# One list schedule for attention and experts, and the carried row added by VectorE

## The chip, the cores and the metric

The kernel runs on one core of one Trainium2 chip. The metric is the device time of one execution in microseconds (us), from a median of several runs. Five engines run side by side, each with a queue of its own that is worked off in order: PE (TensorE, matrix products, with PEld for its weight loads), DVE (VectorE), ACT (ScalarE, functions by tables), POOL (GpSimd) and SP (SyncE, which issues most of the transfers).

## The reference

Inputs are q, k, v, a_re, a_im of shape (4, 8, 768, 48) and the weights of a mixture of 8 experts. First a linear attention with a complex decay per step, head by head:

```python
mag = np.sqrt(a_re * a_re + a_im * a_im)
scale = np.minimum(mag, 0.999) / (mag + 1e-06)
for t in range(S):
    new_re = ar * S_re - ai * S_im
    new_im = ar * S_im + ai * S_re
    S_re, S_im = (new_re + kv, new_im)        # kv = k_t v_t^T
    y[:, :, t] = np.einsum('bhd,bhde->bhe', q[:, :, t], S_re)
```

Its output, seen as x of shape (3072, 384), goes through top-1 experts with a skip test:

```python
do_compute = x @ w_skip > 0
e_idx = np.argmax(xc @ w_gate, axis=1)        # xc = x[do_compute]
h = np.maximum(xc[mask] @ w1[e], 0.0)         # w1[e]: 384 x 1024
y[mask] = gate_w[mask, None] * (h @ w2[e])    # w2[e]: 1024 x 384
out[do_compute] = xc + y
```

## The kernel before

**Attention.** Time is cut into 6 chunks of 128 steps; a unit u is one chunk of one of the 4 batch rows (24 units, u = 4 x chunk + row), always with all 8 heads. The decays become angles and logarithms (`gates`): ScalarE takes Ln and Exp with one table and Arctan and Sin with another, so units are put into batches (`STARTS`) to share table loads. The angle summed up to the end of a chunk is carried: the last row of the reduced angle is moved to partition 0 by a small transfer (L308), GpSimd multiplies it by -2 pi (L312), and GpSimd adds it to the first row of the next chunk's Arctan (L288); then a matrix product with a triangle sums over time. Per unit there follow the products with cos and sin (`w`, L394), transposes (`tp`), copies of them out of PSUM (`wT`, L411; for units 0 to 5 two of four are VectorE's, `SHARE`), scores (`pa`), masked scores (`at`, L441), the state (`st` and `T`, L448 and L461), the output (`py`, `yT`) and its last product (`px`), which puts tokens in rows (`xa`) and gives logits (`lg`).

**Routing.** For each chunk the rank of a token within its expert is found by products with a triangle of ones (`rank`), and the token rows are scattered by an indirect transfer of GpSimd to a table `xs` of 256 rows per expert (`place`, L543). In the last chunk this is done row by row (`route1`), and expert 0 doesn't wait for the table: its tokens are gathered by products with one-hot matrices `ohx`, with the earlier part read back (`early`).

**Order.** `Plan` holds every step of the attention with its engine, its time, its due time, what it needs and which buffers it takes and frees; `Plan.order` is a list scheduler that plays these through and writes one order, and `attention` emits the steps in it, each engine's instruction pinned behind the one before. The experts (`moe`, L859) are written as loops over e, and the framework's own scheduler orders them under a few pins (`issue_after`). Each expert: weights w1 and w2 are loaded (`r`), cast to a high part (`h`, ScalarE, L808) and a low part (`l`, VectorE, L809); tokens `xg` are loaded from `xs` (L826), transposed and split into `xh`, `xl`; 8 x 9 products give `ph` (L889), ReLU splits it into `hh` (ScalarE, L891) and `hl` (VectorE, L892); 2 x 8 x 3 products give `po`; `og` scales and adds (VectorE, L911) and an indirect transfer writes the rows out (L912). A flag (`check`) says whether a fallback is needed.

Of the kernel before, what the change touches and what calls it, by code (L numbers as in the profile page):

```python
# [21 lines left out]
DM = H * D  # L22
# [8 lines left out]
ROOMS = dict(ain=6, tr=5, U=6, cs=2, e=5, qk=4, w0=2, w1=2, wT0=2, wT1=2, vt=3, at=2, st=2, yT=2, row=4, G=1, raw=2,  # L31
             tp=2, pa=2, y=1, g=1, c=2, xa=3)
LEADS = {0: 4.4, 1: 2.53, 2: 4.25, 3: 2.2, 4: 3.8, 5: 3.0, 6: 2.65, 7: 4.06, 8: 4.22}
SHARE = lambda u: ((0, 1), (1, 1)) if u < 6 else ()
# [12 lines left out]
class Plan:  # L47
# [3 lines left out]
    OVER = dict(P=0.0, A=0.085, V=0.085, G=0.0)  # L51
# [4 lines left out]
    def add(self, key, eng, us, at, need=(), take=(), free=()):  # L56
        def put(fn):
            need_ = list(need)
            if (key[0], key[1] - 1) + key[2:] in self.ops and key[0][:2] not in ("rt", "ro"):
                need_.append((None, (key[0], key[1] - 1) + key[2:]))  # L60
            self.ops[key] = (eng, us, at, need_, list(take), fn)
            for x in free:
                self.rel.setdefault(x, []).append(key)
        return put

    def order(self):
        end, free, held, out = {}, dict.fromkeys("PAVGS", 0.0), {"xa": [("xa", "z")]}, []
        pipe, warm = 0.0, [-9.0, 0.0]
        todo = dict(self.ops)

        def ready(eng, need, take):
            t = 0.0
            for x in need:
                x, after = (x[1], False) if x[0] is None else (x, True)
                if x not in end:
                    return None
                f, e, d = end[x]
                t = max(t, d if after and e != eng else f)
            for x in take:
# [7 lines left out]

        while todo:
            can = {}
            for key, (eng, us, at, need, take, fn) in todo.items():  # L90
                r = ready(eng[0], need, take)
                if r is not None:
                    can.setdefault(eng[0], []).append((max(r, free[eng[0]]), at, key))
            assert can, [(k, [y for y in v[3] if y not in end], v[4]) for k, v in todo.items()]
            e, l = min(can.items(), key=lambda x: min(x[1]))
            t0 = min(l)[0] + NEAR
            s, at, key = min((x for x in l if x[0] <= t0), key=lambda x: (x[1], x[0]))
            eng, us, at, need, take, fn = todo.pop(key)
# [16 lines left out]
            out.append((s, key, fn))  # L115
        self.end = end
# [3 lines left out]
class Kern:  # L120
# [108 lines left out]
    def gates(self, u, k, t, end):  # L229
# [18 lines left out]
        @add(("inv", u), "A", 0.54, t, [("ln", u), E], take=[("tr", u)])  # L248
# [4 lines left out]
        @add(("r", u), "V", 0.55, t, [("inv", u)])  # L253
# [3 lines left out]
        @add(("rr", u), "V", 0.63, t, [("r", u)])  # L257
# [4 lines left out]
        @add(("ln1", u), "A", 0.62, t + 0.1, [("rr", u), E])  # L262
# [3 lines left out]
        @add(("sum", u), "V", 0.57, t + 0.1, [("ln1", u)])  # L266
# [4 lines left out]
        @add(("eps", u), "A", 0.62, t + 0.1, [("sum", u), E])  # L271
# [3 lines left out]
        @add(("U", u), "V", 0.55, t + 0.1, [("eps", u)], take=[("U", u)], free=[("ain", u)])  # L275
# [4 lines left out]
        @add(("atan", u), "A", 0.51, t1, [("sum", u), T])  # L280
# [9 lines left out]
        @add(("pt", u), "P", 0.68, t1, [("on" if c else "atan", u)], take=[("c", "pt", u)])  # L290
# [4 lines left out]
        @add(("near", u), "A", 0.485, t1, [("pt", u)])  # L295
# [3 lines left out]
        @add(("y", u), "V", 0.61, t1, [("near", u)], free=[("c", "pt", u)])  # L299
# [4 lines left out]
        if c < NCH - 1:  # L304
# [9 lines left out]
        @add(("abs", u), "V", 0.38, t1, [("y", u)])  # L314
# [3 lines left out]
        @add(("sin", u), "A", 0.52, t1 + 0.1, [("y", u), T], take=[("cs", c)] if b == 0 else [])  # L318
# [5 lines left out]
        @add(("cos", u), "A", 0.61, t1 + 0.1, [("abs", u), ("sin", u), T],  # L324
# [4 lines left out]
        @add(("pl", u), "P", 0.68, t2, [("U", u), ("pt", end - 1)], take=[("c", "pl", u)], free=[("U", u)])  # L329
# [4 lines left out]
        @add(("e0", u), "A", 0.59, t2, [("pl", u), E2], take=[("e", u)])  # L334
# [4 lines left out]
        @add(("e1", u), "A", 0.59, t2, [("e0", u), E2], free=[("c", "pl", u)])  # L339
# [9 lines left out]
    def factors(self, c, t):  # L349
# [3 lines left out]
        @add(("f0", c), "P", 0.25, t, [("dG", c * B + b) for b in range(B)], take=[("g", "f0", c)], free=[("G", c)])  # L353
# [10 lines left out]
        @add(("f2", c), "P", 0.2, t, [("f1", c)], take=[("g", "f2", c)])  # L364
# [8 lines left out]
    def ready(self, u, t):  # L373
# [11 lines left out]
        @add(("qe", u), "V", 0.95, t, [("lq", u), ("e1", u)], free=[("e", u)])  # L385
# [3 lines left out]
        for k in range(2):  # L389
            @add(("w", u, k), "V", 0.95, t, [("qe", u), ("sin", u), ("cos", u)] + ([("w", u, 0)] if k else []),  # L390
# [5 lines left out]
            for hh in range(2):  # L396
                @add(("tp", u, k, hh), "P", 0.45, t, [("w", u, k)], take=[("tp", u, k, hh)], free=[(f"w{k}", u)])
# [8 lines left out]
                @add(("wT", u, k, hh), "V" if onV else "A", 0.68 if onV else 0.587, t, [("tp", u, k, hh)],  # L406
# [10 lines left out]
    def unit(self, u):  # L417
# [12 lines left out]
        for hh in range(2):  # L430
            @add(("pa", u, hh), "P", 0.9, t, [("wT", u, k, hh) for k in range(2)], take=[("pa", u, hh)], free=[("wT1", u)])
# [5 lines left out]
            @add(("at", u, hh), "V", 0.68, t, [("pa", u, hh)], take=[("at", u)], free=[("pa", u, hh)])  # L437
# [6 lines left out]
        if c > 0:  # L444
            @add(("Sb", u), "V", 0.55, t, [("T", u - B), ("f3", c - 1)], take=[("st", u)])
# [4 lines left out]
        if not late:  # L450
            @add(("ps", u), "P", 1.39, t, [("w", u, 1), ("lv", u)], take=[("g", "ps", u)], free=[("w1", u), ("vt", u)])
# [13 lines left out]
        for hh in range(2):  # L465
            @add(("py", u, hh), "P", 1.09 if c else 0.55, t,
# [14 lines left out]
        @add(("yT", u), "A", 0.585, t, [("py", u, 0), ("py", u, 1)], take=[("yT", u)], free=[("y", u)])  # L481
# [6 lines left out]
        @add(("px", u), "P", 0.74, t, [("yT", u), ("wg", 0)], take=[bank], free=[("yT", u)])  # L488
        def _():
            xs = [H // 2, 2 * D + E + 1]  # L490
            px = X["px", u] = self.bank(f"px_{nm}", xs) if late else self.ps_g.tile([128] + xs, F32, name=f"px_{nm}", tag="g")
            for hp in range(H // 2):
                pe = PE.matmul(px[:, hp], X["yT", u][:, hp], self.wg[:, hp], start=True, stop=True)
            self.px_ins = pe.ins
# [13 lines left out]
        @add(("xa", u), "A", 0.485, t, [("px", u), ("lg", u)], free=[bank])  # L508
# [3 lines left out]
        if late or b == B - 1:  # L512
            @add(("ox", u), "S1", 1.0 if late else 4.0, t + 0.3, [("xa", u)], free=[("xa", c)])
# [11 lines left out]
    def chain(self, name, at, steps, *need):  # L525

        last = list(need)
        for i, (eng, us, fn, *more) in enumerate(steps):
            self.plan.add((name, i), eng, us, at, last + list(more))(fn)
            if eng != "A":  # L530
# [83 lines left out]
    def route1(self, c, b, at):  # L614
# [14 lines left out]
        def rank():  # L629
            R["pr"] = self.ps_g.tile([128, E], F32, name=f"pr_{c}_{b}", tag="g")  # L630
            PE.matmul(R["pr"], self.tri, R["oh"], start=True, stop=False)
            self.pr_ins[b] = PE.matmul(R["pr"], self.ones, self.ohs, start=False, stop=True).ins
# [23 lines left out]
        if b == 0:  # L656
            self.plan.add(("early", 0), "S1", 2.0, at, [(f"rt{c - 1}", 19 + B)], take=[("xa", "early")])(self.early)
# [465 lines left out]
```

## Time and profile before

| | us |
|---|---|
| runs: median of 3 | 438.28 (437.83 to 438.39) |
| profiled execution | 437.74, its span 435.5 |
| PE busy, PEld busy | 384.3, 346.2 |
| DVE busy | 325.4 |
| ACT busy | 282.7 |
| POOL busy | 120.6 |

The attention takes the first 280 us and the experts the rest. Busy time of PE is modelled at its ends and matmuls overlap, so a busy PE is not a PE at its peak; that of DVE and ACT is one instruction after the other. "granted clock" (PEclk) is the share of TensorE's full 2.4 GHz that it was given: 1.00 or 0.50 (1.2 GHz), and a mean between them over a stretch with both.

### The profile page before, as it was taken

What the parts mean: (1) busy time and instruction counts of PE and PEld (TensorE: products, weight loads), DVE (VectorE), ACT (ScalarE), POOL (GpSimd) and SP (SyncE); (2) the same over time, 40 slices, a digit from 0 to 9 for tenths busy, and PEclk for the clock granted to TensorE, in tenths of its full rate; (3) what the DMA queues carried; (4) which work ended last, traced back from release to release, by engine and by line L of the source; (5) the groups of instructions that cost most, each with busy time, mean ns of one, the idle gap of its engine ahead of it and who ended that gap; (6) DMA issues with size and microseconds to landing.
All of it is one profiled execution on the core that took longest, in us unless ns stands there. A gap on an engine that the chain in (4) does not pass through costs nothing. (4 is left out here: it accounts for less than half of the span.)

```text
span 435.5 us, 8846 instructions
## 1 busy us (share of the span) xinstructions
PE 384.3 (88%) x3236; PEld 346.2 (79%) x3236; DVE 325.4 (75%) x714; ACT 282.7 (65%) x540; POOL 120.6 (28%) x134
## 2 busy tenths in 40 slices
PE   0557989799999898898999989897899999999993
PEld 0246779588889687687789888896899999999993
DVE  4479999996989989898889866569555857668321
ACT  5798977779799899889876552267345645655120
POOL 7024324403452531572350041201210202012011
PEclk9976999999999999999999999999699999999998
DMA  9999768576749925531485522497746667465000
GB/s 159 186 149 171 130 115 217 206 171 141 143 129 169 145 46 141 90 79 32 129 219 132 175 74 83 129 327 243 244 130 223 195 202 276 149 241 177 2 25 32
DMA packets 148049, 65.55 MB, mean 151 GB/s; under 512 B 129323, under 2 KB 143407, under 8 KB 148000
## 3 DMA queue, kind: packets, MB, share of 16 engines
q1 hardware_dynamic: 145440, 60.29, 57.9%
q0 software_dynamic: 2560, 4.63, 3.0%
q8 instruction: 28, 0.46, 0.5%
q14 instruction: 21, 0.17, 0.1%
HBM read 52.33 MB, written 15.77 MB: 156 GB/s over the span
## 5 line engine op out<-in xcount | busy, mean ns | idle before, releaser
L809 DVE TENSOR_TENSOR l<-r,h 128x768 fp32r<-128x768 f32 (+1 forms) x56 | 58.1, 1068 | 10.0 <-ACT h L808 9.8
L808 ACT CAST h<-r 128x768 fp32r<-128x768 f32 (+1 forms) x56 | 49.9, 925 | 19.0 <-DMA r<-in_moe_w_dram 8.3
L402 PE MATMUL tp<-ident,w 128*96 128x128 f32 x384 | 54.8, 283 | 7.8 <-ACT wT L411 4.9
L889 PE MATMUL ph<-xh,h 128*128 128x256 f32 x192 | 54.2, 288 | 3.5 <-DVE hl L892 3.2
L891 ACT ACTIVATE hh<-ph 128x256 fp32r<-128x256 f32 x64 | 23.4, 380 | 51.8 <-PE ph L889 51.8
L402 PEld LDWEIGHTS tp<-ident,w 128*96 128x96 f32 x384 | 42.9, 131 | 16.1 <-ACT wT L411 6.2
L889 PE MATMUL ph<-xh,l 128*128 128x256 f32 x192 | 54.0, 286 | 0.0
L435 PE MATMUL pa<-wT,wT 96*128 96x128 f32 x384 | 51.4, 280 | 1.8 <-ACT wT L411 1.8
L889 PE MATMUL ph<-xl,h 128*128 128x256 f32 x192 | 52.0, 286 | 0.0
L288 POOL TENSOR_TENSOR tr<-tr,row 1x384 f32<-1x384 f32 x20 | 30.7, 1554 | 73.7 <-ACT tr L222 68.0
L435 PEld LDWEIGHTS pa<-wT,wT 96*128 96x128 f32 x384 | 47.4, 194 | 4.2 <-ACT wT L411 2.2
L411 ACT COPY wT<-tp 96x512 f32<-96x512 f32 x84 | 46.0, 581 | 6.2 <-PE tp L402 6.1
L394 DVE TENSOR_TENSOR w<-qk,cs 128x768 f32<-128x768 f32 x48 | 47.5, 1004 | 0.4 <-PE tp L402 0.2
L892 DVE SCALAR_TENSOR_TENSOR hl<-ph,hh 128x256 fp32r<-128x256 f32 x64 | 25.7, 418 | 29.1 <-ACT hh L891 29.0
L543 POOL DMA_INDIRECT xs<-xa,sl x24 | 29.5, 1229 | 63.4 <-ACT yT L484 38.0
L912 POOL DMA_INDIRECT out_dram<-og,idx x16 | 20.0, 1249 | 91.5 <-DVE og L911 75.3
L906 PE MATMUL po<-h,hh 128*128 128x384 f32 x128 | 43.4, 340 | 0.0
L907 PE MATMUL po<-l,hh 128*128 128x384 f32 x128 | 42.8, 336 | 0.0
L312 POOL TENSOR_SCALAR row<-row 1x384 f32<-1x384 f32 x20 | 28.7, 1434 | 44.2 <-DMA row<-tr 43.4
L908 PE MATMUL po<-h,hl 128*128 128x384 f32 x128 | 40.4, 337 | 0.0
L889 PEld LDWEIGHTS ph<-xh,h 128*128 128x128 f32 x192 | 37.0, 193 | 3.8 <-DVE hl L892 3.4
L476 PE MATMUL py<-at,vt 128*64 128x128 f32 x384 | 37.5, 281 | 2.1 <-ACT tr L222 1.1
(160 smaller groups left out, 853.8 us busy)
## 6 DMA issues: line engine op xcount, KB each, us to landing
r<-in_moe_w_dram SPq DMA_DIRECT2D x24, 512.0 KB
r<-in_moe_w_dram SPq DMA_DIRECT2D x32, 384.0 KB
ain<-in_a_re_dram SPq DMA_DIRECT2D x24, 192.0 KB
ain<-in_a_im_dram SPq DMA_DIRECT2D x24, 192.0 KB
qk<-in_q_dram SPq DMA_DIRECT2D x24, 192.0 KB
qk<-in_k_dram SPq DMA_DIRECT2D x24, 192.0 KB
vt<-in_v_dram SPq DMA_DIRECT2D x24, 192.0 KB
out_dram<-xa SPq DMA_DIRECT2D x5, 768.0 KB
```

Of the source, the lines that this page charges most:

```text
L288: nc.gpsimd.tensor_tensor(first, first, X["row", u - B], ALU.add)
L394: V.tensor_tensor(n, X["qk", u][:, k].unsqueeze(2).to_broadcast([128, H, 2, D]), X["cs", c][:, b], ALU.mult)
L402: nc.tensor.transpose(tp[:, h], n[:, hh * 4 + h].rearrange("p k d -> p (k d)"), self.ident)
L411: (V.tensor_copy if onV else A.copy)(X["wT", u, k][:, hh * 4:hh * 4 + 4], X["tp", u, k, hh])
L435: PE.matmul(pa[:, h % 4], X["wT", u, 1][:, h], X["wT", u, 0][:, h], start=True, stop=True)
L476: PE.matmul(py[j * 64:j * 64 + 64, hp], vt[:, 2 * hp + j], at[:, 2 * hp + j], start=True, stop=(c == 0))
L808: P.append((load, lambda ks=ks, r=r, hi=hi: nc.scalar.copy(hi[:, ks], r[0]), lambda ks=ks, r=r, hi=hi, lo=lo: nc.vector.tensor_tensor(lo[: ...
L809: lambda ks=ks, r=r, hi=hi, lo=lo: nc.vector.tensor_tensor(lo[:, ks], r[0], hi[:, ks], ALU.subtract)))
L889: pe = PE.matmul(ph, w[:, k, js], x[:, k], start=(n == 0), stop=(n == len(terms) - 1))
L906: PE.matmul(po, hh[:, j, sl], w2h[:, j], start=(j == 0), stop=False)
L907: PE.matmul(po, hh[:, j, sl], w2l[:, j], start=False, stop=False)
L908: pe = PE.matmul(po, hl[:, j, sl], w2h[:, j], start=False, stop=(j == NF - 1))
```

## The change

The experts' steps become operations of the same `Plan`: weights, gathers, products, splits, outputs and scatters, the flag's chain and the remainder of the last chunk's routing, each with a time, a due time, its needs and its buffers. `emit` writes the order in two passes, since the experts' pools open when the attention's close, and pins each engine's instruction behind the one before over both. Expert 1's raw weights now use the two buffers of expert 0 and come before the attention's end; from expert 2 on there are four. GpSimd's two operations on the carried row become one of VectorE. The table of numbers is new: 7 batches, other leads, no shared copies (`SHARE` is empty), measured times for many steps; transfers count about half the time.

```diff
-STARTS = [0, 3, 7, 10, 11, 13, 17, 20]
-AHEAD, TRIG, READY, PULL = 3.0, 1.08, 1.49, 2.06
+STARTS = [0, 3, 7, 11, 15, 18, 21]
+AHEAD, TRIG, READY, PULL = 3.0, 0.63, 1.05, 3.44
+WAFTER, WGAP, CHECK = 0.75, 0.21, 2
-SHARE = lambda u: ((0, 1), (1, 1)) if u < 6 else ()
+SHARE = lambda u: ((0, 1), (1, 1)) if u < 0 else ()
...
-            @add(("on", u), "G", 1.4, t1, [("atan", u), ("row", u - B)], free=[("row", u - B)])
+            @add(("on", u), "V", 0.554, t1, [("atan", u), ("mv", u - B)], free=[("row", u - B)])
             def _():
                 first = X["tr", u][0:1, 0]
-                nc.gpsimd.tensor_tensor(first, first, X["row", u - B], ALU.add)
+                V.scalar_tensor_tensor(first, X["row", u - B], -2 * math.pi, first, ALU.mult, ALU.add)
...
-            @add(("row", u), "G", 1.35, t1, [("mv", u)])
-            def _():
-                nc.gpsimd.tensor_scalar(X["row", u], X["row", u], -2 * math.pi, None, ALU.mult)
...
+    def weights(self, e, t, gap, need=(), begin=None):
+        raw_ = "raw" if e < 2 else "raw2"
+        for i in range(KD + NF // 2):
+            old = [] if e < 2 else [("ph", e - 2, NF - 1)] if i < KD else [("po", e - 2, 1, NF - 1)]
+            @add(("wd", e, i), "S1", 1.5 if i < KD else 1.15, t + gap * i, ..., take=[(raw_, e, i)])
+            @add(("wh", e, i), "A", 1.05 if i < KD else 0.835, t + gap * (i + 0.4), [("wd", e, i)] + old)
+            @add(("wl", e, i), "V", 1.22 if i < KD else 0.957, t + gap * (i + 0.4), [("wh", e, i)], free=[(raw_, e, i)])
+
+    def experts(self):
+        T0, TE = n + 1.0, 1.8
+        self.weights(1, n - 1.5, 0.15, [("w", u, 1)])
...
+            te = T0 + TE * e
+            @add(("xg", e), "S1", 1.1, te - 0.9, [("px", u)] + [(f"re{b}", 8) for b in range(B)], take=[("xg", e)])
+                @add(("hl", e, j), "V", 0.418, te + j * 0.11, [("hh", e, j)], free=[("mph", e, j)])
+            if e + 2 < E:
+                self.weights(e + 2, te + WAFTER, WGAP)
+        self.check(T0 + TE * CHECK)
```

What the order is now, at three places. The first is GpSimd and VectorE where the carried row is added for units 11 and following (`tr` is a unit's angles, `row` the carried row, `xs` the scatter of tokens, `T` the state, `qk` a unit's q and k). Before, on POOL:

```order
L288 TENSOR_TENSOR tr_10_995<-tr_10_995,row_6_500 1x384
L543 DMA xs_113<-xa_0_584,sl_0_983 2048x386
L312 TENSOR_SCALAR row_10_1160<-row_10_1160 1x384
L543 DMA xs_113<-xa_0_584,sl_0_983 2048x386
L288 TENSOR_TENSOR tr_11_1198<-tr_11_1198,row_7_904 1x384
L288 TENSOR_TENSOR tr_12_1204<-tr_12_1204,row_8_953 1x384
```

Now, on DVE:

```order
L308 SCALAR_TENSOR_TENSOR tr_11_1113<-row_7_1002,tr_11_1113 1x384
L308 SCALAR_TENSOR_TENSOR tr_12_1193<-row_8_1026,tr_12_1193 1x384
L308 SCALAR_TENSOR_TENSOR tr_13_1237<-row_9_1032,tr_13_1237 1x384
L308 SCALAR_TENSOR_TENSOR tr_14_1287<-row_10_1036,tr_14_1287 1x384
L477 TENSOR_TENSOR T_2_0_1448<-st0_153,ps_2_0_1418 96x384
L322 SCALAR_TENSOR_TENSOR tr_11_1113<-tr_11_1113,col_74,pt_11_1440 128x384
L332 TENSOR_SCALAR tr_11_1113<-tr_11_1113 128x384
L322 SCALAR_TENSOR_TENSOR tr_12_1193<-tr_12_1193,col_74,pt_12_1445 128x384
```

The addition of the row left POOL, whose only work in the body is now the scatters, and four of them stand in a row on DVE ahead of the state sum and the reduced angles (L322) of the same batch.

The second is VectorE at the start of expert 0 (names end in the expert, then j or the part: `l3_1` is the low part of w1 of expert 1, `l8_1` of w2; `xl_0` the tokens' low part; `ok`, `fl` the flag). Before:

```order
L856 TENSOR_TENSOR xl_0_3519<-pt_0_1_3521,xh_0_3518 128x3x128
L809 TENSOR_TENSOR l3_1_3479<-r3_1_0_3482,h3_1_3478 128x1024
L892 SCALAR_TENSOR_TENSOR hl_0_3557<-ph_0_0_3558,hh_0_3556 128x256
L892 SCALAR_TENSOR_TENSOR hl_0_3557<-ph_0_1_3570,hh_0_3556 128x256
L892 SCALAR_TENSOR_TENSOR hl_0_3557<-ph_0_2_3582,hh_0_3556 128x256
L809 TENSOR_TENSOR l3_1_3479<-r3_1_1_3486,h3_1_3478 128x1024
L809 TENSOR_TENSOR l3_1_3479<-r3_1_2_3490,h3_1_3478 128x1024
L892 SCALAR_TENSOR_TENSOR hl_0_3557<-ph_0_3_3594,hh_0_3556 128x256
L809 TENSOR_TENSOR l8_1_3481<-r8_1_0_3494,h8_1_3480 128x768
```

Now:

```order
L815 TENSOR_TENSOR l8_1_3499<-r8_1_3_3476,h8_1_3498 128x768
L688 TENSOR_SCALAR m_5_3_3379<-m_5_3_3379 128x1
L689 RECIPROCAL xa_5_3117<-m_5_3_3379 128x1
L691 SCALAR_TENSOR_TENSOR todo_109<-m_5_3_3379 128x1
L387 COPY Fall_106<-pf_5_3423 96x32
L943 MEMSET ok_3516 128x384
L872 TENSOR_TENSOR xl_0_3513<-pt_0_0_3465,xh_0_3512 128x3x128
L872 TENSOR_TENSOR xl_0_3513<-pt_0_1_3469,xh_0_3512 128x3x128
L956 TENSOR_SCALAR ok_3516<-Fall_106 96x192
L957 TENSOR_SCALAR ok_3516<-Fall_106 96x192
L815 TENSOR_TENSOR l8_1_3499<-r8_1_4_3501,h8_1_3498 128x768
L958 TENSOR_REDUCE fl_3518<-ok_3516 128x1
```

After these come one more split of w2 and then hl_0 for j = 0. The three splits of expert 1's w1 and the first of its w2 moved ahead of expert 0's tokens, and the flag moved from expert 1 to expert 0.

The third is SP's queue there (`r` are raw weights, `xg` tokens from the table). Before, expert 2's tokens stood behind all its weights:

```order
L806 DMA r3_2_0_3732<-in_moe_w1_dram 128x1024
L806 DMA r3_2_1_3736<-in_moe_w1_dram 128x1024
L806 DMA r3_2_2_3740<-in_moe_w1_dram 128x1024
L806 DMA r8_2_0_3744<-in_moe_w2_dram 128x2x384
L806 DMA r8_2_2_3748<-in_moe_w2_dram 128x2x384
L806 DMA r8_2_4_3752<-in_moe_w2_dram 128x2x384
L806 DMA r8_2_6_3756<-in_moe_w2_dram 128x2x384
L826 DMA xg_2_3875<-xs_113 128x2x386
```

Now, from expert 1's second load of w2 on:

```order
L803 DMA r8_1_4_3501<-in_moe_w2_dram 128x2x384
L803 DMA r8_1_5_3510<-in_moe_w2_dram 128x2x384
L850 DMA xg_0_3537<-xs_113 128x2x386
L803 DMA r8_1_6_3550<-in_moe_w2_dram 128x2x384
L803 DMA r3_2_0_3556<-in_moe_w1_dram 128x1024
L850 DMA xg_1_3568<-xs_113 128x2x386
```

Expert 1's tokens now stand behind the first of expert 2's weights, and expert 2's (not shown) behind all of expert 2's and two of expert 3's.

## Rows read from the trace of the kernel before

**Rows 1.** Stages: length, busy us of PE, PEld, DVE, ACT, POOL; PEclk, DMA share, GB/s.

```profile
24.00:60.00 36.00, 28.24 (x188) 22.65 (x189) 34.29 (x60) 32.20 (x64) 15.31 (x11) 0.81 0.83 143
60.00:240.00 180.00, 169.48 (x1642) 144.89 (x1640) 162.22 (x356) 148.75 (x290) 66.29 (x50) 1.00 0.61 136
301.00:315.00 14.00, 9.55 (x58) 9.16 (x57) 9.80 (x22) 5.73 (x12) 4.23 (x3) 0.76 0.79 256
315.00:428.00 113.00, 113.00 (x800) 112.44 (x799) 66.28 (x108) 50.98 (x94) 15.90 (x18) 1.00 0.48 157
```

**Rows 2.** Groups by line, 24 to 262 us: busy us, mean ns | idle before.

```profile
L394 DVE TENSOR_TENSOR w<-qk,cs 128x768 f32<-128x768 f32 x48 | 47.5, 1004 | 0.4 <-PE tp L402 0.2
L411 ACT COPY wT<-tp 96x512 f32<-96x512 f32 x84 | 46.0, 581 | 6.2 <-PE tp L402 6.1
L288 POOL TENSOR_TENSOR tr<-tr,row 1x384 f32<-1x384 f32 x20 | 30.7, 1554 | 73.7 <-ACT tr L222 68.0 <-DVE wT L411 5.7
L741 ACT ACT_TABLE_LOAD x14 | 18.0, 1283 | 0.2
L448 DVE TENSOR_TENSOR st<-T,Fall 96x384 f32<-96x384 f32 x20 | 14.0, 702 | 2.8 <-PE py L479 2.7
L278 DVE SCALAR_TENSOR_TENSOR U<-ain 128x384 f32<-128x384 f32 x21 | 11.3, 548 | 0.0
L411 DVE COPY wT<-tp 96x512 f32<-96x512 f32 x12 | 8.1, 679 | 0.4 <-PE tp L402 0.4
```

**Rows 3.** Timeline around 143 us: start, us, instruction, count.

```profile
142.76 5.85 POOL L288 TENSOR_TENSOR tr<-tr,row 1x384 f32<-1x384 f32 x4 [9.17 <-ACT tr L222]
143.51 2.98 DVE L394 TENSOR_TENSOR w<-qk,cs 128x768 f32<-128x768 f32 x2
146.41 1.35 DVE L448 TENSOR_TENSOR st<-T,Fall 96x384 f32<-96x384 f32 x1
```

**Rows 4.** Timeline at 96 us, DVE.

```profile
96.40 0.95 DVE L394 TENSOR_TENSOR w<-qk,cs 128x768 f32<-128x768 f32 x1
97.27 0.55 DVE L448 TENSOR_TENSOR st<-T,Fall 96x384 f32<-96x384 f32 x1
```

**Rows 5.** Timeline, the end of the attention and the first product of expert 0.

```profile
267.25 0.69 DVE L441 TENSOR_TENSOR at<-pa,mask 128x512 f32<-128x512 f32 x1 [0.72 <-PE pa L435]
...
280.67 0.39 PE L889 MATMUL ph<-xh,h 128*128 128x256 f32 x1 [0.29 <-ACT xh L855]
```

**Rows 6.** Groups by line, 281 to 429 us.

```profile
L889 PE MATMUL ph<-xh,h 128*128 128x256 f32 x192 | 54.2, 288 | 3.5 <-DVE hl L892 3.2 <-ACT xh L855 0.3
L809 DVE TENSOR_TENSOR l<-r,h 128x768 fp32r<-128x768 f32 (+1 forms) x49 | 50.6, 1068 | 8.6 <-ACT h L808 8.4
```

**Rows 7.** Timeline, expert 2's tokens: issue, and the transposes that wait for them.

```profile
302.86 0.37 SPq L826 DMA_DIRECT2D xg<-xs  x1
...
307.54 1.52 PE L842 MATMUL pt<-ident,xg 128*128 128x128 f32 x6 [1.21 <-DMA xg<-xs]
```

**Rows 8.** Busy time by stage, 308 to 312 us.

```profile
308.00:312.00 4.00, 4.00 (x20) 4.00 (x20) 1.88 (x6) 1.35 (x3) 0.00 (x0) 0.50 0.98 380
```

**Rows 9.** Timeline, output steps of experts 4 and 5, two products 1.06 us apart, last product.

```profile
332.40 0.28 PE L889 MATMUL ph<-xh,h 128*128 128x256 f32 x1
333.46 0.28 PE L889 MATMUL ph<-xh,h 128*128 128x256 f32 x1
378.47 0.62 DVE L911 SCALAR_TENSOR_TENSOR og<-po,xg 128x384 f32<-128x384 f32 x1 [1.09 <-PE po L908]
396.01 1.14 DVE L911 SCALAR_TENSOR_TENSOR og<-po,xg 128x384 f32<-128x384 f32 x2 [1.09 <-PE po L908]
428.09 0.34 PE L908 MATMUL po<-h,hl 128*128 128x384 f32 x1
```

**Rows 10.** Timeline, one load of 384 KB: issue, and the cast that waits for it.

```profile
238.31 0.37 SPq L806 DMA_DIRECT2D r<-in_moe_w_dram  x1
...
240.45 0.83 ACT L808 CAST h<-r 128x768 fp32r<-128x768 f32 x1 [1.29 <-DMA r<-in_moe_w_dram]
```

More of the change, by code (lines that the diff above doesn't have):

```diff
@@ L68, in order, with start @@
         pipe, warm = 0.0, [-9.0, 0.0]
-        todo = dict(self.ops)
-        def ready(eng, need, take):
+        left, users, base, todo = {}, {}, {}, set()
+        for key, (eng, us, at, need, take, fn) in self.ops.items():
+            names = {x[1] if x[0] is None else x for x in need}
+            left[key] = len(names)
+            for x in names:
+                users.setdefault(x, []).append(key)
+        def start(key):
+            eng, us, at, need, take, fn = self.ops[key]
             t = 0.0
@@ L74, in ready @@
                 x, after = (x[1], False) if x[0] is None else (x, True)
-                if x not in end:
-                    return None
                 f, e, d = end[x]
-                t = max(t, d if after and e != eng else f)
-            for x in take:
+                t = max(t, d if after and e != eng[0] else f)
+            base[key] = t
+            todo.add(key)
+        def ready(key):
+            t = base[key]
+            for x in self.ops[key][4]:
                 had = held.get(x[0], [])
@@ L115, in order @@
             out.append((s, key, fn))
+            for x in users.get(key, ()):
+                left[x] -= 1
+                if not left[x]:
+                    start(x)
+        assert len(out) == len(self.ops), sorted((k for k in self.ops if k not in end), key=str)[:9]
         self.end = end
@@ L430, in unit @@
         for hh in range(2):
-            @add(("pa", u, hh), "P", 0.9, t, [("wT", u, k, hh) for k in range(2)], take=[("pa", u, hh)], free=[("wT1", u)])
+            @add(("pa", u, hh), "P", 0.91, t, [("wT", u, k, hh) for k in range(2)], take=[("pa", u, hh)], free=[("wT1", u)])
             def _(hh=hh):
@@ L703, in attention, with emit @@
             self.late(0)
-            self.x, self.pr_ins, self.W, self.rests = {}, {}, {}, []
+            self.x = {}
             self.pieces()
-            seen = nc.cur_bb.bb.instructions
-            prev = {}
-            order = self.plan.order()
-            for i, (s, key, fn) in enumerate(order):
-                self.at(24.0 * i / len(order))
-                n0 = len(seen)
-                with ExitStack() as st:
-                    for x in prev.values():
-                        st.enter_context(tc.issue_after(x))
-                    fn()
-                for x in seen[n0:]:
-                    prev[x.engine] = x
-            n = B * NCH
-            self.at(n + 0.5)
-            for r in self.rests:
-                for _ in r:
-                    pass
-            self.at(n + 1)
+            self.order = self.plan.order()
+            self.done, self.prev = {}, {}
+            self.emit(lambda key: key not in self.second)
+    def emit(self, which):
+        seen = self.nc.cur_bb.bb.instructions
+        first, prev = {e: list(v) for e, v in self.done.items()}, {}
+        for i, (s, key, fn) in enumerate(self.order):
+            if not which(key):
+                continue
+            self.at(48.0 * i / len(self.order))
+            n0 = len(seen)
+            with ExitStack() as st:
+                for e in set(first) | set(prev):
+                    before = [x for k, x in first.get(e, ()) if k < i][-1:] + [prev[e] for _ in range(e in prev)]
+                    for x in before:
+                        st.enter_context(self.tc.issue_after(x))
+                fn()
+            for x in seen[n0:]:
+                prev[x.engine] = x
+                self.done.setdefault(x.engine, []).append((i, x))
     def phase_of(self, c):
@@ new lines, in _ @@
+                    for i, (w, x, k) in enumerate(terms):
+                        PE.matmul(ph, w[:, k, ks(j)], x[:, k], start=(i == 0), stop=(i == len(terms) - 1))
+                @add(("hh", e, j), "A", 0.381, te + j * 0.11, [("ph", e, j)], take=[("hh", e)])
+                def _(e=e, j=j):
+                    if ("hh", e) not in X:
+                        X["hh", e], X["hl", e] = [self.hp.tile([128, NF, CAP], F32R, name=f"{a}_{e}", tag=a) for a in ("hh", "hl")]
+                    A.activation(X["hh", e][:, j], X["ph", e, j], AF.Relu)
```

412 lines of the change are left out of this document (196 added, 216 removed).

## The prediction

> **What bounds the kernel now.** I read the busy times by stage first [rows 1]. From 24 to 240 us, the body of the attention, VectorE is busy 34.29 of 36 us and then 162.22 of 180 us (95% and 90%). ScalarE has 32.20 and 148.75 (89% and 83%). TensorE shows 169.48 of 180, but its ends are modelled and its instructions overlap; its weight loads have 144.89 (80%). So I take VectorE as the engine that paces the attention. From 315 us on TensorE is busy all of 113 us: the experts run at its rate, and VectorE (66.28) has room. Between the two stands 301 to 315 us with TensorE busy 9.55 of 14 us at a granted clock of 0.76: that is a hole.
>
> By the Trainium skill, "Perfetto Trace Analysis", section "Identifying the Most-Contended Engine", TensorE's headroom is judged by its weight loads and not by its matmul row, and the busiest engine is the one to relieve. The trace agrees on the first part as far as 80% against 90% can show it; on the second the rule speaks against this change, which puts an operation on that busiest engine.
>
> Second, the groups of the attention by line, with whom each waits for [rows 2], then single instructions in time [rows 3 to 5]. For the hole: what the experts' first products wait for [rows 6, 7], the clock there [rows 8], and the steady period of one expert [rows 9].
>
> **The change, part by part. First the carried row.** GpSimd's two operations for each of 20 units go (L288 alone 30.7 us, mean 1554 ns), and VectorE gets one scalar-times-tensor-plus-tensor of 384 elements for each. Its nearest row is L278, the same form at 128 partitions: 548 ns [rows 2]. That is 20 x 0.548 = +11.0 us on VectorE. Only one partition works, so it could cost less; the bounds are 0.15 us (about what VectorE's smallest operations take, an estimate) and 0.61, so +3 to +12. I take the row of the same length.
>
> Gone too is what GpSimd's operations did to VectorE. A chain of four L288 lasts from 142.76 for 5.85 us; under it two products w took 2.98 us together and the state product st 1.35 [rows 3]. Without GpSimd beside them they take 0.95 and 0.55 [rows 4]. Over the attention the means are 1004 and 702 ns [rows 2]: 48 x 0.054 + 20 x 0.152 = 2.6 + 3.0 = 5.6 us that VectorE loses now. I count all of it as won, -5.6; the bounds are 0 (if the scatters that stay on GpSimd do the same) and -7.
>
> The Trainium skill, "SBUF — State Buffer", section "Who interferes with whom", says why: a VectorE instruction with two SBUF inputs and a GpSimd instruction that reads SBUF take the same port, and the second to issue waits for the whole of the first. The trace agrees: w and st have two SBUF inputs, and 2.98 us for two w of 0.95 holds such a wait.
>
> **Copies.** The 12 transposed copies that VectorE took (L411, 679 ns) go to ScalarE: -8.1 us on VectorE, +12 x 0.581 = +7.0 on ScalarE. Seven batches in place of eight save two table loads, 2 x 1.283 = -2.6 [rows 2]. ScalarE is +4.4 on 180.95 of 216 us; it stays under VectorE, whose work hides it. If that cover is gone the 4.4 us count.
>
> VectorE's sum: +11.0 - 5.6 - 8.1 = **-2.7 us**, taken one to one, since the engine is busy nine tenths (bounds -12 to +4).
>
> **The other order.** Units, loads and batches stand elsewhere on every queue. What this gains or loses the trace of before can't price exactly. A bound: if 60 to 240 us were as full as 24 to 60, VectorE's 17.8 us of idle time would shrink to 9: -9. On the other side the new VectorE operation waits for ScalarE's Arctan, a wait that GpSimd bore 68.0 us of [rows 2]. In the order four of them stand in a row; everything behind them on VectorE (the state sum, the angles, the next masked products) waits too. I take 0 and keep both ends.
>
> **The end of the attention.** From the end of the last masked product (267.25 + 0.69) to the first product of expert 0 (280.67) are 12.7 us [rows 5]. In it TensorE's order was: last px, gathers of rows 0 and 1, ranks of row 2, gather 2, early gather, ranks of row 3, gather 3. Now the ranks of row 2 and gather 0 stand ahead of the last px, and the ranks of row 3 ahead of two gathers, so their wait is filled with gathers. Laid end to end with the durations that the same steps have in this trace (estimates: py 1.9, ranks 0.3, five gathers of about 1.4, px 0.9, copy 0.8, small gaps) I get about 11.3: **-1.4 us** (bounds -3 to +1: two weight splits of 1.2 us now stand in the same stretch of VectorE, ahead of row 3's logits).
>
> **The experts.** From 280.67 [rows 5] to the last product's end at 428.43 are 147.8 us; the steady period is 396.01 - 378.47 = 17.54, eight of them 140.3 [rows 9]. So 7.4 us are lost, all before 315: TensorE stood 3.2 us for VectorE's hl [rows 6], 1.21 for the load of expert 2's tokens, issued at 302.86 [rows 7], and the rest, 3.0, is the half clock after these stalls (0.50 from 308 to 312 [rows 8]). The cause is VectorE's queue: expert 1's splits, which could only start once the attention's buffers were gone, stood between expert 0's activations, and expert 2's and the flag's reductions ahead of expert 1's. In the new order four of expert 1's seven splits stand before expert 0's first xl. What is left: two splits (1.07 us each [rows 6]) and three flag operations ahead of the first hl, which then ends some 4 us after the first product, where the fourth product wants it after 3 x 1.06 = 3.2 (the distance of two hidden columns' first products, 332.40 to 333.46 [rows 9]). I put 0.8 us for that, 0.6 for six later experts at 0.1 (two splits after the output stand ahead of each first hl), and 1.0 for loads that arrive late: expert 1 has two raw buffers, a load of 384 KB took from 238.31 to 240.45, 2.1 us, and a load of tokens 4.7 us, from 302.86 to 307.54 [rows 7, 10]. Together 2.4 in place of 7.4: **-5.0 us** (bounds 0 to -7).
>
> **Sum.** -2.7 - 1.4 - 5.0 = -9.1. The profiled execution took 437.74 us (435.5 of span and 2.2 around it); so 428.6. The median of the runs is 0.5 above it: about **429.1 us**.
>
> **The rivals.** A is the forecast, 424.5 to 433.5.
> B: TensorE paces the attention after all, and VectorE's relief is worth nothing. For it: 169.48 of 180 us busy [rows 1]. Against: VectorE's own stretches without a gap. 437.7 - 6.4 + 0.5 = 431.8.
> C: the order packs VectorE better, up to the -9 above: 420. For it: 24 to 60 us is that full already. Against: that stretch has no routing and no late chunk.
> D: the loads undo the experts' gain. Splits of expert 1 stand ahead of the first hl on VectorE and their casts ahead of it on ScalarE; with two buffers each load starts only when an earlier split is done. At 4.7 us instead of 2.1 for each of two loads the first hl is some 4 to 5 us later, the clock falls again: the gain shrinks to about 0, so 434.
> E, the other side: VectorE waits for Arctan. Six batches carry a row. If VectorE comes to its block when the table load begins, it stands for 1.283 us and the Arctans (an estimate of 0.5 each), some 3 us for four: 6 x 3 = 18, less the 9.1: 447. It decides from 9.1 / 6 = 1.5 us per block on. For it: the 68 us of [rows 2], and the block of four in the order. Against: GpSimd waited because it had nothing else, and ScalarE has the table load well ahead of the block.
>
> **How the numbers follow.** A 0.45, B 0.14, C 0.18, D 0.11, E 0.12. Faster or slower counts beyond 0.2%, 0.9 us, about what runs of this kernel (437.83 to 438.39) can tell. A, B, C are faster, D mostly; 0.83. The near ends of D and E give 0.05 for the same; 0.12 slower. The range, 418 to 438, leaves out the far part of E and of C, and takes in the bounds of VectorE's sum.
>
> **What would show it.** Right: w near 0.95 and st near 0.55 us all through; the new operation near 0.55 and with little wait in front; from first product to last 142 to 143 us, no stretch at half clock after 285 us. Wrong: a wait of VectorE on Arctan over 1.5 us per batch (E); gaps of TensorE ahead of hl or of expert 1's or 2's transposes (D); VectorE less busy than 85% from 60 to 240 with the time unchanged (B). I would be most wrong if the new order left some engine standing at a place that this trace does not have.

## The result and the profile after

The changed kernel takes 425.54 us (median of 4 runs, 425.20 to 426.13) against 438.05 us (435.37 to 438.39): a ratio of 0.973, 95% interval 0.969 to 0.977. The forecast was 429.1 us. The profiled execution took 426.13 us, of which 424.4 are span, so 11.1 us of span went.

First the stages, as in [rows 1]: stretch, length, busy us (instructions) of PE, PEld, DVE, ACT and POOL, granted clock, DMA share, GB/s. The last row is the body of the attention, from 24 us to the end of the last masked product.

```profile
24.00:60.00 36.00, 34.25 (x221) 27.21 (x222) 30.41 (x58) 33.40 (x67) 0.00 (x0) 0.81 0.89 149
60.00:240.00 180.00, 176.00 (x1721) 150.48 (x1720) 162.59 (x384) 151.85 (x303) 22.42 (x20) 1.00 0.62 135
301.00:315.00 14.00, 14.00 (x96) 13.74 (x97) 10.41 (x16) 7.71 (x13) 2.13 (x3) 1.00 0.51 159
24.00:259.68 235.68, 227.56 (x2118) 193.33 (x2120) 210.85 (x505) 196.01 (x388) 28.88 (x27) 0.97 0.67 145
```

The hole at 301 us is gone (14.00 of 14 us, clock 1.00). Before, the body lasted to 267.94 us [rows 5]; the same stretch there, 24.00 to 267.94:

```profile
24.00:267.94 243.94, 224.25 (x2121) 192.10 (x2123) 215.37 (x472) 193.81 (x378) 86.92 (x66) 0.97 0.62 135
```

So the body is 8.3 us shorter: VectorE has 4.5 us less of work (215.4 to 210.9), and its time without work fell by 3.7, from 28.6 to 24.8. The groups behind the 4.5, from 24 to 258 us, which answer to [rows 2]:

```profile
L410 DVE TENSOR_TENSOR w<-qk,cs 128x768 f32<-128x768 f32 x48 | 45.3, 951 | 0.2
L464 DVE TENSOR_TENSOR st<-T,Fall 96x384 f32<-96x384 f32 x20 | 10.9, 548 | 0.5 <-PE py L495 0.5
L308 DVE SCALAR_TENSOR_TENSOR tr<-row,tr 1x384 f32<-1x384 f32 x20 | 10.0, 540 | 0.7 <-ACT tr L242 0.7
L427 ACT COPY wT<-tp 96x512 f32<-96x512 f32 x96 | 52.1, 580 | 2.8 <-PE tp L418 2.6
L332 DVE TENSOR_SCALAR tr<-tr 128x384 int32<-128x384 int32 x21 | 7.6, 361 | 2.0
```

The last of these in the kernel before, from 24 to 262 us:

```profile
L316 DVE TENSOR_SCALAR tr<-tr 128x384 int32<-128x384 int32 x21 | 8.5, 405 | 2.2
```

w fell from 1004 to 951 ns and st from 702 to 548, the values that they have without GpSimd beside them [rows 4]. The new operation takes 540 ns and waited 0.7 us in all 20 places together. VectorE's copies are gone. The step that drops the sign of the reduced angle (L332, before L316) went from 405 to 361 ns. Together these are 10.0 - 8.1 - 2.2 - 3.1 - 0.9 = -4.3 us of the 4.5.

Then the way from the last masked products to expert 0, and to the end:

```profile
258.40 1.28 DVE L457 TENSOR_TENSOR at<-pa,mask 128x512 f32<-128x512 f32 x2
...
270.86 0.39 PE L886 MATMUL ph<-xh,h 128*128 128x256 f32 x1 [0.29 <-ACT xh L868]
...
416.65 0.34 PE L909 MATMUL po<-h,hl 128*128 128x384 f32 x1
```

The end of the attention takes 270.86 - 259.68 = 11.2 us in place of 12.7. The experts take 416.99 - 270.86 = 146.1 in place of 147.8: 1.6 us, where the forecast had 5.0. What TensorE waits for there, from 268 us on, and single waits and transposes of it in time:

```profile
L886 PE MATMUL ph<-xh,h 128*128 128x256 f32 x192 | 54.6, 288 | 1.1 <-DVE hl L896 0.8 <-ACT xh L868 0.3
L862 PE MATMUL pt<-ident,xg 128*128 128x128 f32 x42 | 5.9, 276 | 1.7 <-DMA xg<-xs 1.7
```

```profile
275.69 0.39 PE L886 MATMUL ph<-xh,h 128*128 128x256 f32 x1 [0.78 <-DVE hl L896]
282.44 0.74 PE L862 MATMUL pt<-ident,xg 128*128 128x128 f32 x5 [0.56 <-DMA xg<-xs]
294.30 0.42 SPq L850 DMA_DIRECT2D xg<-xs  x1
301.00 0.85 PE L862 MATMUL pt<-ident,xg 128*128 128x128 f32 x6 [0.55 <-DMA xg<-xs]
330.57 0.28 PE L886 MATMUL ph<-xh,l 128*128 128x256 f32 x1
330.79 0.39 PE L886 MATMUL ph<-xh,h 128*128 128x256 f32 x1
331.01 0.28 PE L886 MATMUL ph<-xl,h 128*128 128x256 f32 x1
355.32 0.85 PE L862 MATMUL pt<-ident,xg 128*128 128x128 f32 x6 [0.36 <-DMA xg<-xs]
373.54 0.85 PE L862 MATMUL pt<-ident,xg 128*128 128x128 f32 x6 [0.20 <-DMA xg<-xs]
```

Three things are to be seen. Each expert takes longer than the steady period of before, 17.54 us [rows 9]: from transposes to transposes 373.54 - 355.32 = 18.2 us, and 17.9 to 18.6 over the others. Expert 2's tokens, issued at 294.30, could be transposed only at 301.00, 6.7 us later. And the rows at 330 us show a loss that stands under no wait: products ph follow each other every 0.12 us, but two here after 0.22.

### The profile page after: what moved, and what is told of

It reads as the page before. It is cut to its first block, busy times and chain, and to the rows that moved or that the text cites. A ratio compares the mean times of both kernels' runs of the same rounds, so it can differ in the third digit from the quotient of the medians.

```text
span 424.4 us, 8790 instructions
## 1 busy us (share of the span) xinstructions
PE 388.5 (92%) x3236; PEld 346.3 (82%) x3236; DVE 319.3 (75%) x722; ACT 283.9 (67%) x550; POOL 56.6 (13%) x94
## 5 line engine op out<-in xcount | busy, mean ns | idle before, releaser
L810 ACT CAST h<-r 128x768 fp32r<-128x768 f32 (+1 forms) x56 | 50.8, 926 | 38.5 <-issue 19.8
L558 POOL DMA_INDIRECT xs<-xa,sl x24 | 28.9, 1206 | 231.3 <-ACT tr L242 85.0
L427 ACT COPY wT<-tp 96x512 f32<-96x512 f32 x96 | 52.1, 580 | 2.8 <-PE tp L418 2.6
L451 PE MATMUL pa<-wT,wT 96*128 96x128 f32 x384 | 52.4, 284 | 0.1
L892 ACT ACTIVATE hh<-ph 128x256 fp32r<-128x256 f32 x64 | 24.3, 383 | 40.1 <-PE ph L886 40.1
L410 DVE TENSOR_TENSOR w<-qk,cs 128x768 f32<-128x768 f32 x48 | 45.3, 951 | 0.2
L909 PE MATMUL po<-h,hl 128*128 128x384 f32 x128 | 43.0, 336 | 0.0
L457 DVE TENSOR_TENSOR at<-pa,mask 128x512 f32<-128x512 f32 x48 | 32.6, 684 | 7.8 <-PE pa L451 7.7
L886 PEld LDWEIGHTS ph<-xh,l 128*128 128x128 f32 x192 | 36.6, 191 | 0.0
L313 PE MATMUL pt<-tr,turns 128*128 128x384 f32 x48 | 22.1, 563 | 15.3 <-ACT tr L242 14.9
```

The costliest lines, as they stand in the source:

```text
L410: V.tensor_tensor(n, X["qk", u][:, k].unsqueeze(2).to_broadcast([128, H, 2, D]), X["cs", c][:, b], ALU.mult)
L427: (V.tensor_copy if onV else A.copy)(X["wT", u, k][:, hh * 4:hh * 4 + 4], X["tp", u, k, hh])
L451: PE.matmul(pa[:, h % 4], X["wT", u, 1][:, h], X["wT", u, 0][:, h], start=True, stop=True)
L457: V.tensor_tensor(X["at", u][:, hh * 4:hh * 4 + 4], X["pa", u, hh], self.mask.rearrange("p (o t) -> p o t", o=1).to_broadcast([128, 4, C]) ...
L810: nc.scalar.copy(X["W", e, n][0][:, ks], X["raw", e, i])
L886: PE.matmul(ph, w[:, k, ks(j)], x[:, k], start=(i == 0), stop=(i == len(terms) - 1))
```

## The experiments

The runs were timed in three groups, each beside the kernel before, whose medians there were 437.62, 438.06 and 438.16 us. Differences marked with a sign are against the changed kernel's 425.54, which was timed beside a 438.05 of the kernel before and not again in these groups: half a microsecond of such a difference can be that of the groups. Stages are those of one profiled execution, which can lie up to 3 us from the median of its run.

**The carried row back on GpSimd, order kept.** `V.scalar_tensor_tensor(first, ...)` becomes `nc.gpsimd.tensor_tensor(...)`, the multiplication stands behind the small transfer; every other instruction is in its place.

```diff
-V.scalar_tensor_tensor(first, X["row", u - B], -2 * math.pi, first, ALU.mult, ALU.add)
+nc.gpsimd.tensor_tensor(first, first, X["row", u - B], ALU.add)
```

> The changed kernel with the carried row back on GpSimd (its two operations), every other instruction in the same place on its engine. Theory 1 (VectorE's busy time paces the attention, and GpSimd's operations cost it nearly what the new operation costs): VectorE loses 20 x 0.54 = 10.8 us and gets back about 7.7 of waits on w and st, so 3 us less of work: 422 to 425. Theory 2 (what the change won is the latency: GpSimd's 1.55 us per row, four in a chain, holds up TensorE's prefix sums and with them each batch): 6 batches of some 1 to 1.5 us, 431 to 435.

Measured: 432.49 us (431.55 to 432.79), +7.0. The body, in the columns of the stages:

```profile
24.00:265.07 241.07, 228.27 (x2118) 193.96 (x2120) 210.55 (x485) 196.76 (x389) 79.98 (x68) 0.96 0.65 142
```

One group of VectorE in it, first with the row on GpSimd, then in the changed kernel:

```profile
L592 DVE TENSOR_TENSOR cand<-lg,mx 128x32 f32<-128x32 f32 x5 | 1.8, 354 | 0.2
```

```profile
L592 DVE TENSOR_TENSOR cand<-lg,mx 128x32 f32<-128x32 f32 x5 | 1.0, 192 | 0.2
```

And the waits along the chain behind the row, from 26 us to the end of the body (us in total, times, longest): the weight load of the prefix sum for the added row, ScalarE's rounding for the sum, VectorE's reduced angle for the rounding. Again with the row on GpSimd and then in the changed kernel:

```profile
PEld pt L313 <- POOL tr L308: 4.2, 5, 1.4
ACT tr L317 <- PE pt L313: 5.0, 10, 1.1
DVE tr L322 <- ACT tr L317: 6.0, 6, 2.4
```

```profile
PEld pt L313 <- DVE tr L308: 1.4, 5, 0.6
ACT tr L317 <- PE pt L313: 1.9, 7, 0.5
DVE tr L322 <- ACT tr L317: 1.9, 3, 0.9
```

VectorE's work is the same, 210.6 against 210.9: the 20 operations that it lost are made up by others that take longer beside GpSimd, small ones too (cand, 354 ns against 192; L332, 440 against 361). The loss is idle time, 30.5 against 24.8, and 4.1 of the 5.7 us are VectorE's wait for the rounding (L322 behind L317), which TensorE's prefix sum and GpSimd's addition precede. Theory 2 holds.

**The copies back on VectorE, order kept.**

```diff
-(V.tensor_copy if onV else A.copy)(X["wT", u, k][...], ...)
+(V.tensor_copy if u < 6 and hh else A.copy)(X["wT", u, k][...], ...)
```

> The changed kernel with 12 of the 24 transposed copies of units 0 to 5 back on VectorE, every instruction in the place that it has on ScalarE in the order. Theory 1 (VectorE paces, as the prediction put it): 12 x 0.68 = 8.1 us more on VectorE, nine tenths of it in the end: 432 to 434. Theory 2 (ScalarE and TensorE are as near to the bound there, so that VectorE's time counts by half or less): 426 to 429.

Measured: 432.36 us (431.40 to 434.01), +6.8; the body is 243.9 us with 217.6 of VectorE's work (+6.7). Theory 1 holds here.

**The old batches and leads.**

```diff
-STARTS = [0, 3, 7, 11, 15, 18, 21]
+STARTS = [0, 3, 7, 10, 11, 13, 17, 20]
```

(with AHEAD to PULL and LEADS of before)

> The changed kernel with the old batches (8) and the old leads, all else as changed (durations, carried row on VectorE, no shared copies, experts in the plan). Theory 1 (the 3.9 us of VectorE's idle time that went, and which the prediction had put at 0, came from the table): two table loads more on ScalarE and those 3.9 us: 429 to 434. Theory 2 (they came from the row and the copies, whatever the table): 425 to 427.

Measured: 431.65 us (430.84 to 432.42), +6.1, in the range of theory 1. But the reason is not the one expected: the body has 215.7 us of VectorE's work (+4.9) and 26.6 of other time. Some 3.7 us of the work are three more splits of weights, which in this order fall ahead of the end of the last masked product, and the experts are 1.0 us shorter (145.1). So of the new table's 6.1 us only 1.8 show as VectorE's idle time; more lies in what the order puts ahead of the attention's end.

**Four accumulators for ph.**

```diff
-mph=3, mpo=3
+mph=4, mpo=2
```

> The changed kernel with four accumulators for ph and two for po in place of three and three. Theory 1 (the experts' steady period is 17.95 in place of 17.54 because VectorE's splits stand ahead of the first hl, and TensorE then waits for an accumulator): the 0.78 us wait in expert 0 and some 0.2 to 0.35 us in each of six experts go, 422.5 to 424. Theory 2 (the longer period has another cause, the late loads of tokens alone, or the wait only moves to po): 425 to 426.

Measured: 426.04 us (423.23 to 427.36), no change that can be told. The waits of TensorE from 270 us on:

```profile
L886 PE MATMUL ph<-xh,h 128*128 128x256 f32 x192 | 53.8, 284 | 0.3 <-ACT xh L868 0.3
L862 PE MATMUL pt<-ident,xg 128*128 128x128 f32 x42 | 5.9, 277 | 3.8 <-DMA xg<-xs 3.7
```

The wait for hl is gone, as theory 1 said, and of the 16 products that followed after about 0.22 us 3 are left; but the wait for tokens grew from 1.7 to 3.7 us. The experts take 146.2 us, as in the changed kernel (146.1). The time was taken by the next one in line, as theory 2 had it.

**Three token buffers**, and then **both**.

```diff
-xg = X["xg", e] = self.xp.tile([128, 2, XW], F32, name=f"xg_{e}", tag="xg")
+xg = X["xg", e] = self.xp.tile([128, 2, XW], F32, name=f"xg_{e}", tag="xg", bufs=3)
-@add(("xg", e), "S1", 1.1, te - 0.9, ...)
+@add(("xg", e), "S1", 1.1, te - 2.3 if e > 1 else te - 0.9, ...)
```

(the tokens' row numbers get a third buffer too; buffers and place in the queue were not tried apart)

> The changed kernel with three buffers for an expert's tokens in place of two (and for their row numbers), so that from expert 2 on the tokens are asked for one expert earlier in SP's queue (two weights behind the place where the expert before was asked for). Theory 1 (the tokens' load, issued when the scatters of the expert two before are done and 6 us under way among 512 KB loads, ends the experts' period): the transposes' waits of experts 2, 5 and 6 (0.55, 0.36 and 0.20 us) and the shorter ones go, 424 to 425. Theory 2 (something else sets the period, the load just fills the time): no change, 425.5.

> The three token buffers and the four accumulators for ph together. With four accumulators alone, TensorE's waits for an accumulator went and those for tokens grew from 1.7 to 3.8 us. Theory 1 (two causes in a row, the second shows when the first is gone): 0.8 us at expert 0 and 0.4 to 0.7 in each of six experts go, periods near 17.6, 421.5 to 423.5. Theory 2 (a third cause behind both, such as the splits on VectorE): periods stay above 17.9, 424.5 to 426.

Measured: 424.14 us (422.96 to 425.21) and 423.28 us (422.36 to 425.30), theory 1 in both. With the buffers alone the waits for tokens fell to 0.4 us and the experts take 143.9 us; with both the wait for hl is gone as well, the later experts' periods are 17.62 us and the experts take 142.6. One wait is left, 1.2 us for expert 1's tokens:

```profile
L862 PE MATMUL pt<-ident,xg 128*128 128x128 f32 x42 | 5.7, 273 | 1.2 <-DMA xg<-xs 1.2
```

**Expert 1's tokens first**, on top of both.

```diff
-te - 2.3 if e > 1 else te - 0.9
+te - 2.3 if e > 1 else te - 1.75 if e < 1 else te - 3.5
```

> Three token buffers and four accumulators as in the run before, and expert 1's tokens asked for right behind expert 0's, ahead of one weight of expert 1 and one of expert 2, after which they stood. The last wait of TensorE in the experts there was 1.20 us for these tokens. Theory 1 (the load waits in the queue behind 0.9 MB of weights): most of it goes, 422 to 423. Theory 2 (it is the last scatter of the attention that lets it start late, and the wait stays): 423 to 424.5.

Measured: 421.08 us (420.43 to 423.74), below both ranges, 4.5 us under the changed kernel and 17 under the kernel before. The wait is gone:

```profile
L862 PE MATMUL pt<-ident,xg 128*128 128x128 f32 x42 | 5.7, 272 | 0.0
```

From the first product (271.42 us) to the end of the last (412.35 + 0.34) the experts take 141.3 us, 1 us above eight of the old periods. This is what the change's plan for the experts could have won: 6.5 us and not 1.6. Of the 2.2 us of this last step the experts show 1.4 (142.6 to 141.3); the last section says where some of the rest lies.

**The kernel before with one edit alone, order kept.** The row as VectorE's operation, and the 12 copies as ScalarE's.

> The kernel before with the carried row alone moved to VectorE (one operation in the place in time where GpSimd's addition stood), all else in the same order. By the prediction's account (VectorE gains 5.6 us of waits and takes on 11.0): 5 us slower, 442 to 444. By what taking it back cost in the changed kernel (7 us, VectorE's work the same, its idle time 5 less): 431 to 434. A third way, that the old order with its place for a 1.4 us operation can't use it: 436 to 438.

> The kernel before with VectorE's 12 transposed copies on ScalarE, each in its place in the order. Theory 1 (VectorE paces, as in the changed kernel, where putting them back cost 6.9 us): 430 to 433. Theory 2 (in the old order ScalarE has two table loads more and stands as near to the bound): 435 to 438.

Measured: 437.66 us (ratio 0.997, 0.995 to 0.999) and 438.03 us (0.999, 0.996 to 1.002). Neither gives what taking it back cost in the changed kernel; the row's time is the third way of its expectation, that of the copies is nearest to theory 2. The body with the copies on ScalarE:

```profile
24.00:268.63 244.63, 227.18 (x2121) 194.19 (x2123) 209.81 (x460) 199.14 (x389) 86.58 (x66) 0.96 0.61 135
```

And the wait of VectorE that grew (2.3 us in the kernel before):

```profile
DVE tr L302 <- ACT tr L297: 5.2, 6, 2.0
```

VectorE's work fell by 5.6 us (215.4 to 209.8) and its other time rose by 6.2 (28.6 to 34.8). That is the forecast's "one to one" tested by itself, in the old order, and it fails. (This profiled execution, 440.72 us, is the slowest of its ten; its body is 0.7 us longer than that of the kernel before.) With the row alone VectorE's work rose by 1.1 us, to 216.5, and its other time stayed (28.9).

**Both edits in the kernel before, order made anew** from its old table and durations:

```diff
-@add(("on", u), "G", 1.4, t1, [("atan", u), ("row", u - B)], ...)
+@add(("on", u), "V", 0.554, t1, [("atan", u), ("mv", u - B)], ...)
-SHARE = lambda u: ((0, 1), (1, 1)) if u < 6 else ()
+SHARE = lambda u: ((0, 1), (1, 1)) if u < 0 else ()
```

> The kernel before with both edits known to its list scheduler: the carried row as one operation of VectorE (0.554 us in the plan) and all copies on ScalarE; the order of the attention is made anew from the old table (8 batches, old leads, old durations), the experts are left to the framework as before. Each edit alone, in the old order, gave 0 to 0.4 us. Theory 1 (they need only an order that knows them): VectorE has 7 us less of work, 431 to 434. Theory 2 (the order is limited by its table and its durations, so that VectorE only stands longer): 436 to 439.

Measured: 435.74 us (ratio 0.994, 0.991 to 0.998): 2.4 us less, and theory 2 is the nearer one. The body has 210.1 us of work and 32.9 of other time: the 5.3 us that VectorE no longer works are mostly spent waiting.

**The same two edits taken back in the changed kernel, order made anew.**

> The changed kernel with the carried row back on GpSimd and the scheduler told so (1.35 and 1.4 us as before), order made anew. With the order left as it was this cost 7.0 us, VectorE's work being the same and its idle time 5.4 us longer. Theory 1 (the 7 us were mostly the price of an order made for another engine): 426.5 to 429. Theory 2 (GpSimd's latency and its port waits can't be planned away): 430.5 to 433.5.

> The changed kernel with 12 copies of units 0 to 5 back on VectorE and the scheduler told so, order made anew from the same table. With the order left as it was this cost 6.9 us. Theory 1 (VectorE's 8.1 us of work count, whatever the order): 430 to 433. Theory 2 (the scheduler makes room for most of it): 426 to 429.

Measured: 436.13 us (433.64 to 438.63), +10.6, and 430.79 us (428.83 to 431.56), +5.3.

```profile
24.00:269.37 245.37, 231.50 (x2118) 196.53 (x2120) 211.94 (x485) 195.00 (x388) 84.83 (x68) 0.95 0.62 137
```

```profile
24.00:264.14 240.14, 228.48 (x2118) 193.62 (x2120) 218.01 (x517) 190.94 (x377) 28.72 (x27) 0.96 0.64 142
```

The first body is that with the row on GpSimd: VectorE has 211.9 us of work and 33.4 of other time, and 436.13 lies above the ranges of both theories. The second is that with the copies on VectorE, 218.0 and 22.1, in the range of theory 1. So an order that knows of the row's place doesn't make it cheaper on GpSimd; here it is dearer. But batches, leads and durations stayed those of the changed kernel, so what a table chosen for the row on GpSimd would give is not shown. The copies' 7.2 us of work are partly made up by less waiting.

## Why the prediction was right, and where it was off

The time lies in the range and in that of the likeliest case, but that it lies so near is partly luck: the body won 8.3 us where the forecast had 2.7, the experts 1.6 where it had 5.0, and the two errors have opposite signs. Nor do the parts add up one by one: taken back alone, the row, the copies and the table cost 7.0, 6.8 and 6.1 us, 19.9 together, where the whole change won 12.5.

- **VectorE's sum, -2.7: measured -4.5 of work.** The terms were right in kind: the new operation 10.0 us (11.0 forecast, 540 ns against 548), the copies gone, w and st at 951 and 548 ns. GpSimd's cost was put too low: with the row alone, in the old order, VectorE's work rose by 1.1 us where the account has 5.4, and taking the row back raised not only w and st but L332 and the small routing operations, and made up for all 20 operations of VectorE.
- **"The other order ... I take 0": measured -3.7** of VectorE's time without work, inside the bounds, and in the direction of rival C at less than half its size. That this is not free is shown by the old kernel with both edits, 435.7: an order made from the old numbers gains 2.4 of the 12.5 us. From there new durations, the experts in the plan and the old table make 431.65, the new table 425.54. How the 4.1 us from 435.74 to 431.65 divide among new durations and the experts in the plan was not tried.
- **"One to one, since the engine is busy nine tenths": held where it was tried in the new order, not in the old.** Copies put back there cost 6.8 us for 6.7 of work; copies taken away in the old order gave nothing for 5.6. One run adds work and the other takes it away, so whether the order or this direction makes the difference is not shown; with the orders made anew, 7.2 us more cost 5.3, and 5.3 less, with the row moved too, gave 2.4.
- **The carried row, +11.0 - 5.6 = +5.4 in the account: the account had its sign wrong.** Back on GpSimd it costs 7.0 us in the same order and 10.6 in one made for it; moved to VectorE in the old order it gained 0.4 us (437.66 against 438.06) where the account has 5.4 lost. The step looked at busy time alone; the row of GpSimd's 68.0 us of waiting for Arctan [rows 2] was read as a wait that VectorE would inherit, when what counted was the work behind it: TensorE's prefix sum, ScalarE's rounding, VectorE's reduced angle, each of which waits longer with the row on GpSimd (1.4 to 4.2, 1.9 to 5.0 and 1.9 to 6.0 us). The Trainium skill, "Perfetto Trace Analysis", section "Identifying the Most-Contended Engine", would have the busiest engine relieved. Here VectorE, the busiest, took on an operation, with its work the same (210.6 and 210.9 us), and the kernel gained 7.0 us. The rule of the Trainium skill, "SBUF — State Buffer", section "Who interferes with whom", that VectorE's operations with two SBUF inputs share a port with GpSimd's reads, agrees with cand, an operation of this kind, at 354 against 192 ns. L332, with one SBUF input, took longer too (440 against 361), which this rule by itself doesn't cover.
- **The tail, -1.4: measured -1.5.**
- **The experts, -5.0: measured -1.6.** The sign "from first product to last 142 to 143 us" did not come: it is 146.1. The hole went as forecast, and the wait left for the first hl had its size (0.8 forecast, 0.78 measured). The step that failed is "0.6 for six later experts at 0.1 ... and 1.0 for loads that arrive late": the periods are 0.3 to 1.0 us over 17.54 in each expert, 3.7 us in the six, and expert 1's tokens came 0.56 us late besides. The experiments show two causes one behind the other: an accumulator that comes free late, and behind it tokens whose load with two buffers is issued only when the scatters of the expert two before are done. That VectorE's splits are what holds the accumulator is read from their place ahead of hl and was not tried by itself. With both removed and expert 1's tokens first, the experts gain 6.5 us.
- **The rivals.** B (TensorE paces) is refuted for the new order by the copies (6.8 us for VectorE's work alone). In the old order its consequence, that VectorE's relief is worth nothing, is what the copies on ScalarE gave; whether TensorE is the reason there stays open. E is refuted: 0.7 us of waits of the new operation. D's signs came, gaps of TensorE ahead of hl (0.78 us) and of expert 1's and 2's transposes (0.56 and 0.55), but they took a part of the gain only, and the clock didn't fall there (1.00 from 285 us on).

## What to carry to other kernels

An operation on a slow engine is priced by the chain that it heads, not by the busy time of the engine that would take it over; putting one piece back, once in the same order and once in an order made anew, separates its price from that of an order made for another engine, as far as the table behind the order suits both. Work moved on or off the busiest engine need not be worth its time, and its price depends on the order around it: the 12 copies gained 0 us when taken away in one order and cost 6.8 when put back in another. When one wait is removed and the time stands still, look for the row that grew by as much, and remove both.

## What was not expected of the hardware

VectorE's operation on 1 partition takes as long as that on 128: 540 ns for 1x384 (L308) against 548 for 128x384 [rows 2]. GpSimd's operations of one partition hold up VectorE's smallest operations most in proportion: 192 to 354 ns.

The granted clock fell at the end of the attention in two of the three runs with three buffers, ahead of the place of their edits. In the run with both, three buffers and four accumulators, it was 0.50 (1.2 GHz) from 262 to 264 us, after TensorE had been busy 2.30 of 4 us, and the end of the attention took 12.3 us. In the last run, with expert 1's tokens first, TensorE was busy 3.40 of 4 us in the same stretch, the clock stayed at 1.00, and the end took 11.2. First the two stretches of the one, then of the other:

```profile
258.00:262.00 4.00, 2.30 (x24) 2.16 (x26) 3.86 (x22) 2.16 (x5) 0.97 (x1) 0.91 0.43 135
262.00:264.00 2.00, 2.00 (x20) 1.70 (x16) 1.52 (x4) 1.12 (x2) 0.00 (x0) 0.50 0.40 144
```

```profile
258.00:262.00 4.00, 3.40 (x44) 3.09 (x45) 3.86 (x20) 2.60 (x4) 0.97 (x1) 1.00 0.53 178
262.00:264.00 2.00, 2.00 (x19) 1.87 (x17) 1.96 (x7) 0.68 (x2) 0.00 (x0) 1.00 0.46 135
```

The two kernels give their engines the same attention in the same order. What differs is one load: ScalarE's cast of a weight waited for it 3.52 us in the one and 2.44 in the other, and TensorE's product px, behind ScalarE's copy of its operand, 1.49 and 0.41:

```profile
256.69 0.83 ACT L810 CAST h<-r 128x768 fp32r<-128x768 f32 x1 [3.52 <-DMA r<-in_moe_w_dram]
259.35 1.14 PE L509 MATMUL px<-wg,yT 128*128 128x105 f32 x8 [1.49 <-ACT yT L500]
```

```profile
255.59 0.83 ACT L810 CAST h<-r 128x768 fp32r<-128x768 f32 x1 [2.44 <-DMA r<-in_moe_w_dram]
258.25 1.14 PE L509 MATMUL px<-wg,yT 128*128 128x105 f32 x8 [0.41 <-ACT yT L500]
```

Behind it the masked products ended 1.1 us later, and the end of the attention, with the clock at 0.50 in part of it, took 1.1 us more. Why the load landed later stays open. In the run with four accumulators alone the same two waits were 3.25 and 1.23 us and the clock stayed at 1.00. The profiled execution with the fall, 425.30 us, is the longest of its five, whose mean clock was 0.974 against 0.980 to 0.992 in the others, so how much of the step from the median 423.28 to 421.08 is load and clock, and not the tokens, can't be told.
